# A planner's lengths, weight places and queue order in an attention, MLP and expert kernel

## The chip, the cores and the metric

The kernel runs on one core of a Trainium2 chip. The metric is the device time of one execution in microseconds (us); the time before is 1440.73 us, the median of three runs (1438.99 to 1442.17).

## The reference

Three layers follow each other. Everything is float32.

```
# 1. attention through 32 packed queries, for each of 8 batches x 8 heads (576 tokens, 64 wide)
p_packed = sm_attn(p, k, v)                  # sm_attn: softmax(scale * a @ b.T) @ c
out = sm_attn(q, p_packed, p_packed)
x = out.transpose(0, 2, 1, 3).reshape(4608, 512)
# 2. MLP, 512 -> 2048 -> 512
h = x @ w_in
x = (h * tanh(softplus(h))) @ w_out
# 3. experts: each token goes to the best of 8
logits = x @ w_gate
e_idx = argmax(logits); gate_w = softmax(logits)[e_idx]
eom = sigmoid(x @ w_output_gate)
out[token] = gate_w * eom[e_idx] * (relu(x @ w1[e_idx]) @ w2[e_idx])
```

The weights `w_in` and `w_out` come as 64-bit floats (4 MB and 4 MB of float32 content, loaded as two 32-bit words each) and are converted on the chip into float32 values or into a rounded high and a low part.

## The kernel before, in words

**An order made by a planner.** The program is not written in the order in which it runs. Each step is handed to a class `Order` (line 32) by `od.op(engine, length, function, reads, writes, ...)`. `Order.run` (line 132) is a list scheduler: it keeps a time for each engine, takes among the steps whose inputs are made the one that can start first (a tie goes to the lower `prio`, then to the older step), and calls its function, which emits the instructions. The length, a landing time `lat` for DMAs and a hop of 0.18 us between engines are the only things that it knows of time. They are not waits in the program: the result is one fixed list of instructions for each engine, and the waits among them come from the data. Each engine works its list in order, so an instruction whose input is late holds back all that stands behind it on that engine. Where a step may run on ScalarE or VectorE (a dict of lengths), the planner chooses the engine too. Steps carry a group number; a step more than `AHEAD` = 3 groups in front of the oldest unfinished group is held back.

`Order.place` (line 100) gives each buffer one of the places of its tag, the one that comes free first. Places of different tags may overlap in memory; a place is taken only when every buffer that overlaps it has been read for the last time. The weight words have eight places `raw`, in the memory that the packed products `wp` use later.

When the planner sees TensorE pause between two steps, `Order.fill` (line 117) puts filler matmuls (function `busy`, line 432 in the profile) into the pause, one for each 0.25 us, on a bank that is free. Their results are not used.

**The stages.** A *unit* (function `unit`, line 498) is the attention of four heads of one batch: 16 units, two for each batch. It loads K, the packed queries (two DMAs), V and Q over SP's queue, transposes K on TensorE (`heads_T`), forms the scores of the packed queries, takes their softmax (line 584 is the Exp on ScalarE), multiplies by V, and then the second softmax over the 32 packed keys. Unit 1 has buffers and PSUM banks of its own (5 and 6); all other units share one set (banks 0 and 1) and follow each other. Line 535 is the first transpose of a unit, line 637 the transpose after which the packed result `pt_b` is known, line 731 its last matmuls.

`convert` (line 762) loads a block of weights (512 KB) over SP (line 772), one step on ScalarE (line 779), four on VectorE (788, 791, 797, 803), and sums on TensorE (821 to 824). There are 32 such blocks, four for each of four column groups of `w_in` (`i`) and of `w_out` (`o`).

`packed(b)` (line 844) multiplies the packed result of batch b with `w_in`: four matrices (line 855) one after another through one buffer `wq`, which takes banks 0 and 1 together. Each is then evacuated in four steps (two high parts, two low parts) into two of the eight places `wp`.

`block(j)` (line 876) is one of 18 blocks of 256 tokens, each with eight *pairs* (`pair`, line 889): a first product (line 909 from the packed matrices, line 900 for the two blocks of leftover tokens), the activation in nine steps on ScalarE, VectorE and GpSimd (913, 916, 944, 948, 954), and a second product (line 930). Batch b uses blocks `FIRST[b]` and `FIRST[b] + 1`. `route` then chooses the expert of each token (its count matmul is line 1029) and stores the rows.

`slot` (line 1213) is one of 16 slices of 288 tokens of one expert: rows gathered, expert weights loaded over SP and split (1273, 1276), products 1328, 1362 and 1370, and the scatter of the result. They begin near 960 us.

**What sets the order around the change.** `LO` lists the loads of SP's queue by preference (`u` the five loads of a unit, `c` a block of `convert`). `UAT` gives the group of each unit, `CPR` the priority of the steps of each four blocks of `convert`. Units have priority -2 to -4, `packed` -1, the first product of a pair 0 and the second 1.

Of the kernel before, what the change touches and what calls it, by code (L numbers as in the profile page):

```python
# [14 lines left out]
AF = mybir.ActivationFunctionType  # L15
# [174 lines left out]
def tile_attn_moe_moe(  # L190
# [36 lines left out]
    CW = 512  # L227
# [93 lines left out]
    def banks(*n):  # L321
# [18 lines left out]
        tab0=area(PT, 264), tab1=area(XT + 1024, 720), zero=area(ROW, E * CAP // 128),  # L340
        xl0=area(XL, 1024), xl1=area(XT + 1024, 1024), wp=area(WP, 1024, 8), raw=area(WP, 1024, 8), wq=[(("b", 0, 1), ("b", 1, 1))],
        Lx=area(WP + 8192 - LS, LS), tu=area(CT, 512, 2), ts=area(CT + 1024, 512, 4),
# [136 lines left out]

    left, at_b, pt_b = {}, {}, {}  # L480
# [10 lines left out]

    LO = ('u u' + 16 * ' c' + 8 * ' c' + ' u' + 8 * ' c' + ' u').split()

# [4 lines left out]
    def unit(u):  # L498
# [5 lines left out]
        def buf(tag):  # L504
            return od.buf(f"{tag}{x}")
# [20 lines left out]

        op("SP", 1.65, lambda: f_ld(k, kn), w=[kn], lat=LAND, at=start)
        for c in range(2):
            op("SP", 0.3, lambda c=c: f_pn(c), m=[pn], lat=LAND, at=start)
        op("SP", 1.65, lambda: f_ld(v, vn), w=[vn], lat=LAND, at=start)  # L530
        op("SP", 1.65, lambda: f_ld(q, qn), w=[qn], lat=LAND, at=start)
# [63 lines left out]
        for r in range(2):  # L595
            op("DVE", 0.38, lambda r=r: f_mx(r), r=[sc], w=[mx])
        op("DVE", 0.13, f_mm, w=[mx])
# [90 lines left out]
        for c in range(2):  # L688
# [3 lines left out]
            op("DVE", d, lambda c=c: f_sub(c), r=[s2[c], sm], w=[a2])  # L692
        op("ACT", 0.65, lambda: A.activation(out=a2.t, in_=a2.t, func=AF.Exp, scale=scale), w=[a2])
        op("DVE", 1.27, f_sum, r=[a2], w=[sm])
        op("Pool", 1.23, lambda: nc.gpsimd.tensor_tensor(
            out=a2.t, in0=a2.t, in1=gb(sm.t[:, 1]), op=ALU.mult), r=[sm], w=[a2])
# [4 lines left out]
        for c in (1, 0):  # L701
# [12 lines left out]
            else:  # L714
# [47 lines left out]
    def convert(n, srcs, dst, part, after=(), at=0.0, prio=0):  # L762

        cc, wb = od.buf("cc"), dst if part else od.buf("raw")

# [43 lines left out]
        lo = at_in("c", n)  # L809
        od.op("SP", 1.46, f_ld, w=[wb], lat=2.0, after=after, at=at, prio=prio if lo is None else lo - 100)  # L810
# [33 lines left out]
    def packed(b):  # L844

        for m in range(DFF // CW):
# [12 lines left out]

            od.op("PE", 0.95, f_w, r=[pt_b[b, 0], pt_b[b, 1]] + [wi_b[h][m] for h in range(4)], w=[wq], prio=WPR)  # L860
            for g in range(2):
# [10 lines left out]

                od.op(dict(ACT=0.48, DVE=0.6), None, f_hi, r=[wq], w=[wp], prio=WPR)
                od.op("DVE", 0.6, f_lo, r=[wq], w=[wp], prio=WPR)

# [13 lines left out]
    def pair(j, i, i0, i1, acc):  # L889
# [49 lines left out]
        else:  # L939
            need = [x for g in range(2) for x in (at_b[b, g], wp_b[b, i // 2, g])]  # L940
        last["g1", j] = od.op("PE", 3.5 if b is None else 1.31, f_g1, r=need, w=[hps], prio=0, after=())
        if b is not None and half and i == KF // 2 - 1:
            free_at[b] = [last["g1", j]]
        od.op("ACT", 0.49, lambda: A.activation(  # L944
            out=tl(tu, [128, 2, TB]), in_=hps.t, func=AF.Tanh, scale=0.5), r=[hps], w=[tu])
        od.op("ACT", 0.53, f_ts, r=[tu], w=[ts])
        od.op("ACT", 0.53, lambda: sq(tu.t, ts.f, QA, QB), r=[ts], w=[tu])
        od.op("ACT", 0.53, lambda: A.activation(out=tu.t, in_=tu.t, func=AF.Exp, bias=QC), w=[tu])  # L948
        od.op("DVE", 0.61, lambda: stt(ts.f, ts.f, 0.5, tu.t), r=[tu], w=[ts])
        od.op("ACT", 0.53, lambda: sq(ts.f, ts.f, 1.0, -1.5), w=[ts])  # L950
        od.op("DVE", 0.61, lambda: stt(ts.f, ts.f, 0.75, tu.t), r=[tu], w=[ts])
        od.op("DVE", 0.61, lambda: stt(ts.f, ts.f, -1.0, hps.t), r=[hps], w=[ts])
# [3 lines left out]
        last["g2", j] = od.op("PE", 2.59, f_g2, r=[g, ts] + wo_b[2 * i:2 * i + 2], w=[acc], prio=1, after=left[final(1)] if j == 0 and i == 0 else ())  # L956

    def route(j, acc, part):
# [254 lines left out]
    def slot(od, mem, j, dram_b, marks, early=False):  # L1213
# [70 lines left out]
        for i in range(8):  # L1284
            op("SP", 1.5, lambda i=i: f_raw(i), "x0", r=[tab[0]], w=[raw[i]], lat=4.0)
        for i in range(8):
            late = 0 if i > 3 else 0.0
            op("ACT", 0.96, lambda i=i: f_wh(i), r=[raw[i]], w=[ws[i]], pen=pen + late)
            op("DVE", 1.14, lambda i=i: f_wl(i), r=[raw[i]], w=[ws[i]], pen=pen + late)

# [3 lines left out]
        for kk in range(KD):  # L1294
# [208 lines left out]
```

## Time and profile before

| | us |
|---|---|
| median of three runs | 1440.73 |
| the profiled execution | 1453.15 |
| its span (first to last instruction) | 1451.4 |
| TensorE busy | 1394.5 |
| VectorE busy | 1040.5 |
| ScalarE busy | 845.4 |
| GpSimd busy | 413.3 |

The profile is of one execution. PE is TensorE's matmuls, PEld its weight loads, DVE is VectorE, ACT ScalarE, POOL GpSimd, and SP the engine whose queue issues most DMAs. L930 is line 930 of the kernel. Filler counts as busy time of PE. PEclk is the granted clock of TensorE as a share of its full speed. "Idle before, releaser" names the instruction that a waiting one waited for last.

### The profile page before, as it was taken

The page shows a single profiled execution, that of the slowest core. Times are in us where ns is not written, and L with a number is a line of the kernel's source. Part 1 is how long each engine was busy: PE and PEld are TensorE (multiplying, and loading weights), DVE is VectorE, ACT ScalarE, POOL GpSimd, SP SyncE. Part 2 cuts the span into 40 slices and gives each one's busy share as a digit, 9 for nine tenths or more (in the row PEclk, how much of TensorE's full clock was granted, in tenths as well). Part 3 has the DMA queues.
Part 4 walks back from the last instruction along what each step waited for, and adds up shares of the span by engine and source line. Part 5 has one row for each costly group of instructions (what it writes and reads, how often), then busy time and mean ns, then how long its engine had stood idle before and what let it go on. Part 6 is the DMA issues. An engine that isn't in the chain of part 4 may idle for free.

```text
span 1451.4 us, 25837 instructions
## 1 busy us (share of the span) xinstructions
PE 1394.5 (96%) x9594; PEld 1094.8 (75%) x9594; DVE 1040.5 (72%) x2312; ACT 845.4 (58%) x1631; POOL 413.3 (28%) x388
## 2 busy tenths in 40 slices
PE   7789999999999999999999999999999999999997
PEld 4457676777876787887678788778778788878886
DVE  4789777787866856885787887767677767767653
ACT  3568555786756756775777777654354444435432
POOL 1122032233322323332233333431432223223111
PEclk9999999999999999999999999999999999999999
DMA  9871123212223103132210121543654664565430
GB/s 243 206 199 27 35 50 70 62 34 48 41 55 70 34 17 50 16 66 61 57 16 18 16 15 16 147 88 140 198 209 157 194 228 165 177 219 194 150 141 27
DMA packets 70134, 143.61 MB, mean 99 GB/s; under 512 B 13552, under 2 KB 32112, under 8 KB 70000
## 3 DMA queue, kind: packets, MB, share of 16 engines
q1 hardware_dynamic: 61680, 122.92, 32.1%
q0 software_dynamic: 8320, 18.96, 3.9%
q8 instruction: 77, 1.26, 0.5%
q14 instruction: 57, 0.47, 0.1%
HBM read 122.77 MB, written 19.08 MB: 98 GB/s over the span
## 4 chain that ended last, share of the span: by engine, by line
PE 69%; DVE 12%; issue 7%; ACT 5%; DMA 4%; POOL 1%; another core or an unknown queue 1%; SPq 0%; POOLq 0%; DVEq 0%; ACTq 0%
PE b L930 22%; PE b L1328 11%; PE b L1362 10%; PE b L909 9%; DVE f L916 5%; PE b L900 3%; DMA f<-in_moe_w_in_dram 2%; ACT f L913 2%; PE b L855 2%; PE b L1299 2%; PE b L1370 2%; PE b L547 2%; PE b L432 1%; PE b L980 1%; PE b L564 1%
## 5 line engine op out<-in xcount | busy, mean ns | idle before, releaser
L930 PE MATMUL b<-r,r 128*128 128x512 f32 x1728 | 430.3, 400 | 4.9 <-POOL r L954 4.9
L930 PEld LDWEIGHTS b<-r,r 128*128 128x128 f32 x1728 | 317.4, 189 | 80.3 <-issue 8.4
L954 POOL TENSOR_TENSOR r<-f,r 128x512 fp32r<-128x512 f32 x144 | 199.5, 1386 | 468.6 <-ACT r L440 216.6
L913 ACT ACTIVATE f<-f 128x512 f32<-128x512 f32 x432 | 264.6, 628 | 87.2 <-DVE f L916 56.2
L916 DVE SCALAR_TENSOR_TENSOR f<-f,f 128x512 f32<-128x512 f32 x288 | 234.0, 817 | 77.1 <-ACT f L913 44.7
L1328 PE MATMUL b<-r,r 128*128 128x288 f32 x1536 | 213.6, 297 | 4.8 <-issue 3.3
L1328 PEld LDWEIGHTS b<-r,r 128*128 128x128 f32 x1536 | 208.9, 190 | 9.3 <-issue 4.7
L909 PE MATMUL b<-r,r 128*128 128x256 f32 x1536 | 206.8, 286 | 3.1 <-DVE f L916 2.9
L909 PEld LDWEIGHTS b<-r,r 128*128 128x128 f32 x1536 | 189.0, 190 | 24.3 <-DVE f L916 8.8
L1362 PE MATMUL b<-r,r 128*128 128x512 f32 x768 | 191.8, 399 | 0.0
L1362 PEld LDWEIGHTS b<-r,r 128*128 128x128 f32 x768 | 140.3, 188 | 37.2 <-issue 7.5
L1276 DVE TENSOR_TENSOR r<-f,r 128x1024 fp32r<-128x1024 f32 x128 | 157.3, 1241 | 10.3 <-ACT r L1273 7.7
L440 ACT ACTIVATE f<-b 128x288 f32<-128x288 f32 (+5 forms) x229 | 101.2, 464 | 71.4 <-PE b L637 20.4
L1273 ACT ACTIVATE r<-f 128x1024 fp32r<-128x1024 f32 x128 | 132.7, 1056 | 12.8 <-DMA f<-in_moe_w_dram 8.9
L1389 POOL DMA_INDIRECT out_dram<-f,f x48 | 51.2, 1066 | 286.6 <-ACT f L1378 164.7
L944 ACT ACTIVATE f<-b 128x512 f32<-128x512 f32 x144 | 85.1, 591 | 59.6 <-DVE f L916 28.8
L1335 ACT ACTIVATE r<-b 128x288 fp32r<-128x288 f32 x95 | 38.8, 410 | 117.3 <-PE b L1328 99.0
L916 DVE SCALAR_TENSOR_TENSOR f<-f,b 128x512 f32<-128x512 f32 x144 | 98.2, 683 | 3.5
L948 ACT ACTIVATE f<-f 128x512 f32<-128x512 f32 x144 | 90.5, 628 | 2.5
L440 ACT ACTIVATE r<-b 128x512 fp32r<-128x512 f32 (+1 forms) x119 | 59.3, 509 | 37.6 <-PE b L824 12.6
L442 DVE COPY f<-b 128x288 f32<-128x288 f32 (+5 forms) x115 | 57.8, 516 | 32.7 <-PE b L564 17.2
L1378 ACT ACTIVATE f<-b,f 128x512 f32<-128x512 f32 x26 | 17.9, 688 | 94.9 <-PE b L1362 90.1
(181 smaller groups left out, 1638.5 us busy)
## 6 DMA issues: line engine op xcount, KB each, us to landing
f<-in_moe_w_dram SPq DMA_DIRECT2D x128, 512.0 KB
xr<-f SPq DMA_DIRECT2D x36, 257.0 KB
f<-in_k_dram SPq DMA_DIRECT2D x16, 576.0 KB
f<-in_v_dram SPq DMA_DIRECT2D x16, 576.0 KB
f<-in_q_dram SPq DMA_DIRECT2D x16, 576.0 KB
f<-in_moe_w_in_dram SPq DMA_DIRECT2D x32, 256.0 KB
f<-in_moe_w_out_dram SPq DMA_DIRECT2D x16, 512.0 KB
f<-in_p_dram SPq DMA_DIRECT2D x32, 32.0 KB
```

The costliest lines, as they stand in the source:

```text
L440: A.activation(out=dst, in_=src, func=AF.Copy)
L909: nc.tensor.matmul(t[:, c, :], lhsT=wt, rhs=xx, start=(n == 0), stop=(n == 5))
L913: A.activation(out=out, in_=in_, func=AF.Square, scale=sc, bias=b)
L916: V.scalar_tensor_tensor(out=out, in0=in0, scalar=s, in1=in1, op0=ALU.add, op1=ALU.mult)
L930: nc.tensor.matmul(acc.t[t], lhsT=gg[:, c, sl], rhs=wo_at(f, ww), start=(f == 2 * i0 and n == 0), stop=(f == 2 * i1 - 1 and n == 2),)
L944: od.op("ACT", 0.49, lambda: A.activation(out=tl(tu, [128, 2, TB]), in_=hps.t, func=AF.Tanh, scale=0.5), r=[hps], w=[tu])
L948: od.op("ACT", 0.53, lambda: A.activation(out=tu.t, in_=tu.t, func=AF.Exp, bias=QC), w=[tu])
L954: od.op(LOE, None, lambda eng: either(eng).tensor_tensor(out=ts.t, in0=ts.f, in1=g.t.bitcast(F32), op=ALU.subtract), r=[g], w=[ts])
L1273: A.activation(out=wpart(i, 0), in_=raw[i].t, func=AF.Copy)
L1276: V.tensor_tensor(out=wpart(i, 1), in0=raw[i].t, in1=wpart(i, 0).bitcast(F32), op=ALU.subtract)
L1328: nc.tensor.matmul(t, lhsT=ww[:, sl], rhs=xpart(x)[:, kk], start=(n == 0), stop=(n == 3 * KD - 1))
L1362: nc.tensor.matmul(bank(ps), lhsT=h[x], rhs=w[y], start=(f == 0 and n == 0), stop=(f == KE - 1 and n == 2))
```

## The change

Most lengths that the planner is given become longer, and one (a copy on VectorE) shorter; a load on SP is booked by its size, 2.13 us for 512 KB and 2.35 us for 576 KB, and lands 7 us later (`LAND`) where weight loads had 2 us before. Weight blocks that belong to the first two column groups of `w_in` may take four more places, in the memory of the last two column groups. The order of the blocks, the order of the loads on SP and the priorities of the blocks change; unit 3 moves to group 0. From batch 2 on, the first transposes of a unit (packed queries, K and Q) are ordered behind the last matrix of `packed` of the batch in front, and units of later groups are handed to the planner after `packed`. The numbers and shapes of the instructions stay.

```diff
@@ slots
-  raw=area(WP, 1024, 8), wq=...
+  raw=area(WP, 1024, 8), raw0=area(WI + 4096, 1024, 4) + area(WP, 1024, 8), wq=...
@@ lengths (us)
-    HIE = {'ACT': 0.53, 'DVE': 0.6}
-    HR = dict(ACT=0.09, DVE=0.1)
-    YO = dict(ACT=0.57, DVE=0.6)
-    LOE = {'Pool': 1.24}
+    HIE = {'ACT': 0.63, 'DVE': 0.56}
+    HR = dict(ACT=0.19, DVE=0.19)
+    YO = dict(ACT=0.68, DVE=0.7)
+    LOE = {'Pool': 1.38}
-    EV = dict(ACT=0.3, DVE=0.38)
+    EV = dict(ACT=0.44, DVE=0.48)
@@ order of loads on SP
-    LO = ('u u' + 16 * ' c' + 8 * ' c' + ' u' + 8 * ' c' + ' u').split()
+    LO = ('u u' + 16 * ' c' + 8 * ' c' + 8 * ' c' + ' u u').split()
@@ unit
-        op("SP", 1.65, lambda: f_ld(k, kn), w=[kn], lat=LAND, at=start)
+        op("SP", 2.35, lambda: f_ld(k, kn), w=[kn], lat=LAND, at=start)
...
+        begun = made.get(b - 1, ()) if b > 1 else ()
         op("PE", 0.12, lambda: nc.tensor.transpose(bank(pt)[:, 0:128], ...),
-           r=[pn], w=[pt])
+           r=[pn], w=[pt], after=begun)
...
-                op("PE", 0.25, f, r=[src], w=[t_ps])
+                op("PE", 0.25, f, r=[src], w=[t_ps], after=begun)
@@ convert
-        cc, wb = od.buf("cc"), dst if part else od.buf("raw")
+        early = [wi_b[kk][m] for kk in range(KD) for m in range(2)]
+        cc, wb = od.buf("cc"), dst if part else od.buf("raw0" if dst in early else "raw")
...
-        od.op("SP", 1.46, f_ld, w=[wb], lat=2.0, ...)
-        op("ACT", 0.53, f_a1, r=[wb], w=[cc])
-        op("DVE", 0.34, f_b1, w=[cc])
-        op("DVE", 0.61, f_sg, w=[cc])
-        op("DVE", 0.34, f_pw, w=[cc])
-        op("DVE", 0.61, f_lw, r=[wb], w=[cc])
+        od.op("SP", 2.13, f_ld, w=[wb], lat=LAND, ...)
+        op("ACT", 0.67, f_a1, r=[wb], w=[cc])
+        op("DVE", 0.43, f_b1, w=[cc])
+        op("DVE", 0.69, f_sg, w=[cc])
+        op("DVE", 0.43, f_pw, w=[cc])
+        op("DVE", 0.69, f_lw, r=[wb], w=[cc])
@@ packed
-            od.op("PE", 0.95, f_w, ..., w=[wq], prio=WPR)
+            made[b] = [od.op("PE", 0.95, f_w, ..., w=[wq], prio=WPR)]
@@ pair
-        last["g1", j] = od.op("PE", 3.5 if b is None else 1.31, f_g1, ...)
+        last["g1", j] = od.op("PE", 3.5 if b is None else 1.39, f_g1, ...)
...
-        last["g2", j] = od.op("PE", 2.59, f_g2, ...)
+        last["g2", j] = od.op("PE", 2.78, f_g2, ...)
@@ slot
-            op("SP", 1.5, lambda i=i: f_raw(i), "x0", ..., lat=4.0)
+            op("SP", 2.13, lambda i=i: f_raw(i), "x0", ..., lat=4.0)
...
-            cop("PE", 1.475, f_g1, "g1", r=[xx] + ws[0:4], w=[ps])
+            cop("PE", 1.6, f_g1, "g1", r=[xx] + ws[0:4], w=[ps])
@@ the loop over blocks
-    UAT = [0, 0, 0, 1, 2, 2, 4, 4, 6, 6, 8, 8, 11, 11, 13, 13]
+    UAT = [0, 0, 0, 0, 2, 2, 4, 4, 6, 6, 8, 8, 11, 11, 13, 13]
...
-        for u in units.get(j, ()):
-            od.group = j
-            unit(u)
         if j == 0:
+            for u in units[0]:
+                od.group = j
+                unit(u)
             od.group = None
-            n, CPR = 0, [0, 0, 0, 0, 1, 1, 1, 1]
-            for kind, m in [(x, m) for m in range(DFF // CW) for x in 'io']:
+            n, CPR = 0, [0] * 8
+            for kind, m in [('i', 0), ('i', 1), ('o', 0), ('i', 2), ('o', 1), ('i', 3), ('o', 2), ('o', 3)]:
...
         if j in PAT:
             packed(PAT[j])
+        for u in units.get(j, ()) if j else ():
+            unit(u)
```

## Rows read from the trace of the kernel before

**Rows 1.** The page's busy time of each engine: us (share of the span) xinstructions.
```profile
PE 1394.5 (96%) x9594; PEld 1094.8 (75%) x9594; DVE 1040.5 (72%) x2312; ACT 845.4 (58%) x1631; POOL 413.3 (28%) x388
```

**Rows 2.** Stages, all instructions: from:to, length, busy us of each engine, clock, DMA.
```profile
22.70:56.30 33.60, 30.20 (x279) 16.52 (x279) 30.72 (x66) 17.09 (x37) 4.76 (x6) 0.95 1.04 277
...
62.10:84.00 21.90, 21.62 (x165) 13.64 (x165) 19.76 (x45) 17.48 (x37) 3.68 (x2) 0.88 0.84 210
84.00:88.90 4.90, 0.02 (x2) 0.02 (x1) 4.90 (x10) 2.60 (x5) 4.83 (x1) 0.87 1.01 306
88.90:110.00 21.10, 21.10 (x109) 15.21 (x109) 14.20 (x30) 11.88 (x23) 1.94 (x2) 0.87 0.58 147
...
204.00:262.00 58.00, 55.75 (x451) 37.61 (x450) 41.40 (x119) 32.27 (x70) 12.58 (x12) 1.00 0.26 52
262.00:417.00 155.00, 153.03 (x1227) 122.53 (x1226) 122.84 (x272) 117.18 (x234) 53.20 (x45) 1.00 0.23 47
417.00:462.00 45.00, 42.70 (x358) 29.21 (x357) 27.75 (x74) 25.16 (x54) 9.58 (x10) 1.00 0.30 67
...
650.00:706.00 56.00, 53.78 (x429) 37.41 (x428) 35.10 (x89) 32.88 (x70) 11.79 (x11) 1.00 0.26 60
...
1064.00:1400.00 336.00, 336.00 (x2060) 280.75 (x2059) 234.95 (x456) 154.19 (x279) 90.36 (x87) 1.00 0.55 185
```

**Rows 3.** The same for line 432 (filler) alone: busy us of PE and PEld.
```profile
0.00:110.00 110.00, 22.26 (x79) 7.72 (x79) 0.91 0.87 216
...
204.00:262.00 58.00, 10.87 (x42) 3.86 (x42) 1.00 0.26 52
262.00:417.00 155.00, 0.98 (x4) 0.12 (x2) 1.00 0.23 47
417.00:462.00 45.00, 7.38 (x28) 2.58 (x28) 1.00 0.30 67
...
650.00:706.00 56.00, 7.38 (x28) 2.59 (x28) 1.00 0.26 60
...
sum 1451.40, PE 56.15 PEld 18.96; mean PE 7.02 PEld 2.37
```

**Rows 4.** Waits of TensorE up to 200 us: us in total, times, longest.
```profile
PE b L731 <- DVE f L442: 5.8, 1, 5.8
PE b L607 <- ACT f L584: 5.7, 1, 5.7
PE b L930 <- POOL r L954: 4.9, 1, 4.9
```

**Rows 5.** ScalarE in order of time near 21 us: start, length, what, idle before.
```profile
21.48 0.66 ACT L779 ACTIVATE f<-f 128x512 f32<-128x512 f32 x1 [5.51 <-DMA f<-in_moe_w_in_dram]
22.04 0.48 ACT L584 ACTIVATE f<-b,f 128x288 f32<-128x288 f32 x1
```

**Rows 6.** Waits of SP's queue up to 130 us: total, times, longest.
```profile
SPq L772 <- DVE r L803: 24.6, 5, 12.8
SPq L523 <- PE b L535: 23.8, 2, 18.8
```

**Rows 7.** TensorE in order of time, unit 4's first transpose, then 248 to 257 us.
```profile
174.68 0.27 PE L535 MATMUL b<-ident,f 128*128 128x128 f32 x1
...
248.41 1.59 PE L855 MATMUL b<-f,f 64*32 64x512 f32 x16
249.94 2.12 PE L432 MATMUL b<-ones 128*128 128x512 bf16 x9
251.98 1.37 PE L855 MATMUL b<-f,f 64*32 64x512 f32 x16
253.28 3.01 PE L909 MATMUL b<-r,r 128*128 128x256 f32 x24
```

**Rows 8.** Lines 731 and 1029: min/median/max ns, first and last start in us.
```profile
L731 PE MATMUL b<-f,f x128: 222/222/368, 45.9 to 812.7; 128*64 128x64 f32 x128
L1029 PE MATMUL b<-f,tri x18: 166/179/180, 209.7 to 1016.1; 128*128 128x8 bf16 x18
```

More of the change, by code (lines that the diff above doesn't have):

```diff
@@ L340, in tile_attn_moe_moe @@
         tab0=area(PT, 264), tab1=area(XT + 1024, 720), zero=area(ROW, E * CAP // 128),
-        xl0=area(XL, 1024), xl1=area(XT + 1024, 1024), wp=area(WP, 1024, 8), raw=area(WP, 1024, 8), wq=[(("b", 0, 1), ("b", 1, 1))],
+        xl0=area(XL, 1024), xl1=area(XT + 1024, 1024), wp=area(WP, 1024, 8), raw=area(WP, 1024, 8), raw0=area(WI + 4096, 1024, 4) + area(WP, 1024, 8), wq=[(("b", 0, 1), ("b", 1, 1))],
         Lx=area(WP + 8192 - LS, LS), tu=area(CT, 512, 2), ts=area(CT + 1024, 512, 4),
@@ L477, in f_wgl @@
         )
-    left, at_b, pt_b = {}, {}, {}
+    left, at_b, pt_b, made = {}, {}, {}, {}
     xl_b = [od.buf(f"xl{i}") for i in range(2)]
@@ L525, in f_pn @@
             )
-        op("SP", 1.65, lambda: f_ld(k, kn), w=[kn], lat=LAND, at=start)
+        op("SP", 2.35, lambda: f_ld(k, kn), w=[kn], lat=LAND, at=start)
         for c in range(2):
-            op("SP", 0.3, lambda c=c: f_pn(c), m=[pn], lat=LAND, at=start)
-        op("SP", 1.65, lambda: f_ld(v, vn), w=[vn], lat=LAND, at=start)
-        op("SP", 1.65, lambda: f_ld(q, qn), w=[qn], lat=LAND, at=start)
+            op("SP", 0.5, lambda c=c: f_pn(c), m=[pn], lat=LAND, at=start)
+        op("SP", 2.35, lambda: f_ld(v, vn), w=[vn], lat=LAND, at=start)
+        op("SP", 2.35, lambda: f_ld(q, qn), w=[qn], lat=LAND, at=start)
+        begun = made.get(b - 1, ()) if b > 1 else ()
         pt, bd = buf("pp"), buf("bd")
         op("PE", 0.12, lambda: nc.tensor.transpose(bank(pt)[:, 0:128], pn.t.rearrange("p c d -> p (c d)"), ident),
-           r=[pn], w=[pt])
+           r=[pn], w=[pt], after=begun)
         op(dict(ACT=0.16, DVE=0.2), None, lambda eng: evac(eng, tl(bd, [128, 128]), pt.t[:, 0:128]), r=[pt], w=[bd])
@@ L595, in unit @@
         for r in range(2):
-            op("DVE", 0.38, lambda r=r: f_mx(r), r=[sc], w=[mx])
+            op("DVE", 0.45, lambda r=r: f_mx(r), r=[sc], w=[mx])
         op("DVE", 0.13, f_mm, w=[mx])
@@ L692, in unit @@
             op("DVE", d, lambda c=c: f_sub(c), r=[s2[c], sm], w=[a2])
-        op("ACT", 0.65, lambda: A.activation(out=a2.t, in_=a2.t, func=AF.Exp, scale=scale), w=[a2])
+        op("ACT", 0.73, lambda: A.activation(out=a2.t, in_=a2.t, func=AF.Exp, scale=scale), w=[a2])
         op("DVE", 1.27, f_sum, r=[a2], w=[sm])
-        op("Pool", 1.23, lambda: nc.gpsimd.tensor_tensor(
+        op("Pool", 1.39, lambda: nc.gpsimd.tensor_tensor(
             out=a2.t, in0=a2.t, in1=gb(sm.t[:, 1]), op=ALU.mult), r=[sm], w=[a2])
@@ L809, in convert @@
         lo = at_in("c", n)
-        od.op("SP", 1.46, f_ld, w=[wb], lat=2.0, after=after, at=at, prio=prio if lo is None else lo - 100)
-        op("ACT", 0.53, f_a1, r=[wb], w=[cc])
-        op("DVE", 0.34, f_b1, w=[cc])
-        op("DVE", 0.61, f_sg, w=[cc])
-        op("DVE", 0.34, f_pw, w=[cc])
-        op("DVE", 0.61, f_lw, r=[wb], w=[cc])
+        od.op("SP", 2.13, f_ld, w=[wb], lat=LAND, after=after, at=at, prio=prio if lo is None else lo - 100)
+        op("ACT", 0.67, f_a1, r=[wb], w=[cc])
[3 more added lines that the diff above has]
+        op("DVE", 0.69, f_lw, r=[wb], w=[cc])
         cv = od.buf("cv")
@@ L858, in f_w @@
                         )
-            od.op("PE", 0.95, f_w, r=[pt_b[b, 0], pt_b[b, 1]] + [wi_b[h][m] for h in range(4)], w=[wq], prio=WPR)
+            made[b] = [od.op("PE", 0.95, f_w, r=[pt_b[b, 0], pt_b[b, 1]] + [wi_b[h][m] for h in range(4)], w=[wq], prio=WPR)]
             for g in range(2):
@@ L871, in f_lo @@
                     )
-                od.op(dict(ACT=0.48, DVE=0.6), None, f_hi, r=[wq], w=[wp], prio=WPR)
-                od.op("DVE", 0.6, f_lo, r=[wq], w=[wp], prio=WPR)
+                od.op(dict(ACT=0.59, DVE=0.68), None, f_hi, r=[wq], w=[wp], prio=WPR)
+                od.op("DVE", 0.68, f_lo, r=[wq], w=[wp], prio=WPR)
     def block(j, i0=0, i1=KF // 2):
@@ L940, in pair @@
             need = [x for g in range(2) for x in (at_b[b, g], wp_b[b, i // 2, g])]
-        last["g1", j] = od.op("PE", 3.5 if b is None else 1.31, f_g1, r=need, w=[hps], prio=0, after=())
+        last["g1", j] = od.op("PE", 3.5 if b is None else 1.39, f_g1, r=need, w=[hps], prio=0, after=())
         if b is not None and half and i == KF // 2 - 1:
             free_at[b] = [last["g1", j]]
-        od.op("ACT", 0.49, lambda: A.activation(
+        od.op("ACT", 0.6, lambda: A.activation(
             out=tl(tu, [128, 2, TB]), in_=hps.t, func=AF.Tanh, scale=0.5), r=[hps], w=[tu])
[L946 to L952, printed above, removed]
+        od.op("ACT", 0.63, f_ts, r=[tu], w=[ts])
+        od.op("ACT", 0.63, lambda: sq(tu.t, ts.f, QA, QB), r=[ts], w=[tu])
+        od.op("ACT", 0.63, lambda: A.activation(out=tu.t, in_=tu.t, func=AF.Exp, bias=QC), w=[tu])
+        od.op("DVE", 0.77, lambda: stt(ts.f, ts.f, 0.5, tu.t), r=[tu], w=[ts])
+        od.op("ACT", 0.63, lambda: sq(ts.f, ts.f, 1.0, -1.5), w=[ts])
+        od.op("DVE", 0.77, lambda: stt(ts.f, ts.f, 0.75, tu.t), r=[tu], w=[ts])
+        od.op("DVE", 0.69, lambda: stt(ts.f, ts.f, -1.0, hps.t), r=[hps], w=[ts])
         last["hi", j] = od.op(HIE, None, lambda eng: evac(eng, tl(g, [128, 2, TB], F32R), ts.f), r=[ts], w=[g])
@@ L955, in pair @@
             out=ts.t, in0=ts.f, in1=g.t.bitcast(F32), op=ALU.subtract), r=[g], w=[ts])
-        last["g2", j] = od.op("PE", 2.59, f_g2, r=[g, ts] + wo_b[2 * i:2 * i + 2], w=[acc], prio=1, after=left[final(1)] if j == 0 and i == 0 else ())
+        last["g2", j] = od.op("PE", 2.78, f_g2, r=[g, ts] + wo_b[2 * i:2 * i + 2], w=[acc], prio=1, after=left[final(1)] if j == 0 and i == 0 else ())
     def route(j, acc, part):
@@ L1284, in slot @@
         for i in range(8):
-            op("SP", 1.5, lambda i=i: f_raw(i), "x0", r=[tab[0]], w=[raw[i]], lat=4.0)
+            op("SP", 2.13, lambda i=i: f_raw(i), "x0", r=[tab[0]], w=[raw[i]], lat=4.0)
         for i in range(8):
             late = 0 if i > 3 else 0.0
-            op("ACT", 0.96, lambda i=i: f_wh(i), r=[raw[i]], w=[ws[i]], pen=pen + late)
-            op("DVE", 1.14, lambda i=i: f_wl(i), r=[raw[i]], w=[ws[i]], pen=pen + late)
+            op("ACT", 1.06, lambda i=i: f_wh(i), r=[raw[i]], w=[ws[i]], pen=pen + late)
+            op("DVE", 1.23, lambda i=i: f_wl(i), r=[raw[i]], w=[ws[i]], pen=pen + late)
         def xpart(x):
@@ L1311, in slot @@
             cop(EV, None, f_xh, "dx", r=[ps], w=[xx], front=True)
-            cop("DVE", 0.38, f_xl, r=[ps], w=[xx], front=True)
+            cop("DVE", 0.45, f_xl, r=[ps], w=[xx], front=True)
         hT, hr = [], od.buf("hr")
```

12 lines of the change are left out of this document (6 added, 6 removed).

## The prediction

> **What bounds the kernel now.** I read the busy shares first. TensorE counts as busy for 1394.5 us of the span of 1451.4, VectorE for 1040.5, ScalarE for 845.4 [rows 1]; so a new order of the same work can win only what TensorE does not spend on work. That has two parts: idle time, and the filler matmuls of line 432, which the planner puts into every pause that it foresees on TensorE; they took 56.15 us in all [rows 3]. 1451.4 − (1394.48 − 56.15) = 113 us without work. Then the stage table with all instructions [rows 2] against the same stages with the filler alone [rows 3]: idle time of TensorE is the stage less its busy time, and idle plus filler is dead time.
> - From 1064 to 1400 TensorE has no idle moment in 336 us [rows 2]; nothing can be won there.
> - The stretches 204–262, 417–462 and 650–706 hold 2.25 + 10.87 = 13.1, 2.30 + 7.38 = 9.7 and 2.22 + 7.38 = 9.6 us of dead time: 32.4 in 159 us. The stretch between the first two holds 1.97 + 0.98 = 2.95 in 155 us; two others like it lie behind (462–650, 706–904).
> - The first 110 us hold three true stalls of TensorE, 5.7, 5.8 and 4.9 us [rows 4], and stages with a granted clock of 0.95, 0.88 and 0.87 [rows 2].
>
> What ended the waits says why. At 22 us TensorE waits for the second Exp of unit 0 (line 584), and that instruction stands on ScalarE behind a weight conversion (line 779), which sat 5.51 us until its words landed [rows 5]: the planner had booked a weight load at 1.46 us plus 2.0 to land. At 62 us it is the same with line 442 on VectorE, behind line 788. In SP's queue, loads of raw weight words wait 24.6 us in all for line 803 to free a place, 12.8 us once, and unit 3's packed queries wait up to 18.8 us for unit 2's transpose [rows 6] with every later load behind them. In the dead stretches the PE rows show filler between the matrices of `packed` (line 855), and the pairs that need them (line 909) only after the last [rows 7]. Attention has priority -2, `packed` -1, and a `wq` takes banks 0 and 1 together, which attention takes one by one.
>
> **The change, part by part.** The trace is of an execution of 1453.15 us, 12.4 above the median of 1440.73. I work out savings in its time and take them off the median; 0.9% of a saving of tens of us is nothing.
>
> *Lengths.* The program has the same instructions, and no length is a wait: they only steer the planner. The new ones stand near the rows (line 779 is booked at 0.67 instead of 0.53; it took 0.66 [rows 5]). Where TensorE never idles (1064–1400) the order was already good enough; I put this at 0 there. Elsewhere longer chains in the model can show it more pauses and so more filler: from −8 us (the filler outside the first 110 us and the three bad stretches: 56.15 − 22.26 − 25.63 [rows 3]) to +10 (as much again). I take 0, the nearer stages being smooth.
>
> *Loads by bytes, landing 7 us, four more raw places, new load order.* This is the first 110 us. The stall up to 22.7 (5.7 us [rows 4]) goes, since the planner now books the first words late and lets the Exp go first; but the unit then waits sooner for its own next step: I count 4. The stall up to 62.1 (5.8) goes whole: all 32 weight blocks now stand on SP ahead of the five loads each (K, two of the packed queries, V, Q) of units 2 and 3, so nothing of unit 3 blocks that queue, and the twelve places (eight before) take the first eight blocks of `w_in` at once. Of the 4.9 us at 84–88.9 I count 1.9 only, for VectorE was busy in all of it [rows 2]: there it is the engine that bounds, and 32 conversions of about 2.2 us on it (4 steps at 0.43 and 0.69, as booked now) are 72 us that no order removes. The clock lost 33.6 × 0.05 + 21.9 × 0.12 + 21.1 × 0.13 = 7.0 us of work in the stages behind the stalls; I count 3.3 back. Sum 15.0. Against it: unit 2 is loaded behind eight more weight blocks (4 MB) than before, and `packed` of batch 1 needs units 2 and 3; and with CPR all zero a late weight block no longer yields to pairs. Bounds for that: 0 (unit 3 had all 32 in front of it before too) and 5.8 (one more stall like that at 56 us); I take 4, nearer the stall, since VectorE has no slack to catch up. **First term: 11 us** less, bounds 0 and 23.3 (16.3 of stalls and 7.0 of clock).
>
> *Attention behind the matrix in front.* `begun` makes the transposes of unit 2b and 2b+1 wait, in the planner, for the last matrix of batch b−1. It is an order on TensorE's queue and adds no instruction. Unit 3 is made in group 0 instead of 1, which only lifts a limit. The order takes away what held `wq` back. At the rate of the smooth stretch, 2.95/155, the 159 us of the three bad stretches would have 3.0 dead, so 29.4 are in excess. Of those about half lie between the matrices themselves: each next one waits until four evacuations of about 0.6 us have emptied both banks, and that stays when no pair is at hand. So 14.7. What waits now: both units of a batch, and behind them `packed` of the same batch, which needs the second unit up to about two fifths of its chain. Units follow each other at (812.7 − 45.9)/15 = 51 us, blocks at (1016.1 − 209.7)/17 = 47 [rows 8]; 1.4 units are 72 us and two blocks 95, so it fits with 23 us to spare. I take 1.7 off for the tight ones. **Second term: 13 us** less, bounds 29.4 less and 40 more (below).
>
> Sum: 11 + 13 = 24; 1440.7 − 24 = **1417 us**.
>
> One rule of the Trainium skill speaks against the second term (TensorE: Matmul & The Clock Gate, section "HAM oscillation — how this bites in real kernels"): a kernel that lets TensorE wait long in each round starts each round on the slow clock. The trace agrees: behind the stall at 56–62 the granted clock was 0.88, that is partly at 1.2 GHz, while the bad stretches, with filler in their pauses, kept 1.00 [rows 2, 3]. It is the last rival below.
>
> **Rivals.**
> - *Only the start is won* (0.17): the dead time between the matrices is the emptying of banks 0 and 1 and not attention in front. For it: in rows 7 the filler lies between two matrices with nothing of attention between. Against it: the smooth transitions empty the same banks. 1440.7 − 11 = 1430 us.
> - *All stalls go* (0.10): 23.3 + 29.4 less, and some filler back: about 1392 us. Against it: VectorE is full at the start.
> - *Nothing moves* (0.08): VectorE sets the start whatever the order, and what the transitions give, new filler takes: 1441 us, within 0.2% (2.9 us, about what a measurement can tell from no change).
> - *Attention comes late* (0.15), the slower side: one mechanism, the same `begun`. From the point where 1.4 units last longer than the two blocks in which they must run (units of 68 us, against 51 now), `packed` is late at every batch. For it: no unit may now begin before the last matrix, where before some began some 77 us ahead (unit 4 at 174.7, against the matrix at 252 [rows 7]); against it the 23 us to spare. Price: the second term is lost, and the four smooth transitions get an excess of half a bad one each (29.4/3/2 = 5) to a whole one: +20 to +40; with the first term 1450 to 1470 us; say 1452.
> - *Pauses without filler* (0.05): the model sees no pause where there still is one, so none is filled, and the clock falls at each of seven transitions. By the row at 62–84 a fall costs 2.6 us of work: +18 − 11, 1448 us.
>
> **How the numbers follow.** Forecast as reasoned 0.45, with its own range 1400 to 1430. Faster by over 0.2%: 0.45 + 0.17 + 0.10 = 0.72; within 0.2%: 0.08; slower: 0.15 + 0.05 = 0.20. The range to hold 8 in 10 leaves out the end of "all stalls go" and the dear half of "attention comes late": 1396 to 1450.
>
> **What would show it.** In the first term: no wait of TensorE over 4 us before 100 us, both Exps of unit 0 ahead of the first line 779 on ScalarE, SP's wait for line 803 well under 24.6 us, no granted clock under 0.9 in a stage after 30 us. In the second: the four matrices of each batch from 1 on within about 20 us, no unit's first transpose ahead of the last matrix of the batch in front, filler from 200 to 900 us under 12 us (it is 27 or so now). It would be wrong if line 855 waits for line 442 or 637 of a late unit, if TensorE idles more than now between 200 and 900, or if the stretch behind 1064 lengthens.

## The result, and the profile after

The changed kernel takes 1415.62 us (median of four runs, 1414.34 to 1416.88), against 1439.86 us of the kernel before, measured beside it; the ratio is 0.9827, 95% interval 0.9803 to 0.985. The forecast was 1417 us.

The page of the changed kernel, busy time of each engine, answers to [rows 1]. TensorE is busy for 98% of a span that is 36 us shorter. The kernels' work is the same, but the planner moved 60 instructions from ScalarE to VectorE, and there is more filler: 65.7 us instead of 56.1 in the two traces compared below.

```profile
PE 1385.3 (98%) x9646; PEld 1089.7 (77%) x9646; DVE 1057.3 (75%) x2372; ACT 826.3 (58%) x1571; POOL 424.3 (30%) x388
```

Some 12 of these 36 us are not the change's. The kernel before took 1443 us on two of the chips and 1457 us on another; the trace that the prediction read (1453.15 us) is like the slower one. Its stretch behind the last count matmul (1016 to the end) lasted 435 us, where a second trace of the same kernel has 427. So I read the terms from two traces taken on one chip, the kernel before again (1441.18 us) and the changed one again (1419.92 us, the slowest of its four executions). Their spans differ by 21.3 us; by medians on that chip the two kernels differ by 27.0 us.

Stages of the kernel before: up to the count matmul of block 0, from there to that of block 17, and the rest; all instructions, then the filler alone. Columns as in [rows 2].

```profile
0.00:207.70 207.70, 182.83 (x1300) 121.71 (x1301) 158.75 (x330) 122.44 (x244) 42.45 (x62) 0.95 0.53 133
207.70:1012.60 804.90, 790.12 (x5740) 620.99 (x5740) 597.88 (x1399) 540.06 (x1051) 252.01 (x213) 1.00 0.26 52
1012.60:1439.50 426.90, 416.32 (x2557) 348.69 (x2556) 282.78 (x585) 182.41 (x336) 119.45 (x113) 0.99 0.52 175
...
0.00:207.70 207.70, 24.00 (x85) 8.21 (x85) 0.95 0.53 133
207.70:1012.60 804.90, 29.89 (x112) 10.14 (x112) 1.00 0.26 52
1012.60:1439.50 426.90, 2.21 (x7) 0.60 (x7) 0.99 0.52 175
```

The same stages of the changed kernel:

```profile
0.00:199.20 199.20, 189.45 (x1366) 120.70 (x1367) 169.39 (x342) 126.27 (x249) 39.05 (x61) 1.00 0.51 133
199.20:986.60 787.40, 776.60 (x5712) 620.12 (x5710) 601.91 (x1438) 517.25 (x995) 253.53 (x215) 1.00 0.28 54
986.60:1418.20 431.60, 420.05 (x2572) 349.66 (x2571) 285.27 (x593) 182.26 (x328) 129.12 (x113) 0.99 0.53 173
...
0.00:199.20 199.20, 37.29 (x144) 13.29 (x144) 1.00 0.51 133
199.20:986.60 787.40, 22.48 (x90) 8.13 (x90) 1.00 0.28 54
986.60:1418.20 431.60, 5.96 (x22) 1.74 (x22) 0.99 0.53 173
```

| us | before: length, idle + filler, clock | changed |
|---|---|---|
| to block 0 | 207.7, 24.9 + 24.0 = 48.9, 0.95 | 199.2, 9.8 + 37.3 = 47.0, 1.00 |
| to block 17 | 804.9, 14.8 + 29.9 = 44.7, 1.00 | 787.4, 10.8 + 22.5 = 33.3, 1.00 |
| the rest | 426.9, 10.6 + 2.2 = 12.8, 0.99 | 431.6, 11.6 + 6.0 = 17.5, 0.99 |

Dead time is idle time plus filler. The reader is to see three things. In the first stage the idle time fell by 15.1 us and the filler rose by 13.3: the dead time is nearly the same, and what was won is the clock. A clock of 0.95 on 207.7 us loses 10.4 us, which is an upper bound for the work, since it counts idle time and filler too; busy time without filler fell by 6.6 us, from 158.8 to 152.2, though the changed kernel does a little more work there (1222 matmuls, where 1215 were). In the second stage the dead time fell by 11.4. In the third it rose by 4.7, as the stage did. Dead time and clock together (106.3 to 97.8 us; a mean clock of 0.989 on 1439.5 us lost 15.8, one of 0.995 on 1418.2 loses 7.1) give 17.2 of the 21.3 us. The other 4 us I can't place: the second stage's busy time without filler fell by 6.1 us at a clock that both rows show as 1.00.

Each stage ends at the same instruction, but the planner moves other work across that point; so between versions dead time can be compared by stage, and the length of a stage only where about as many matmuls stand in it.

What ended the waits has changed too. ScalarE near 16 us in the first trace of the changed kernel (start, length): all Exps of units 0 and 1 (line 585 now) stand ahead of the first conversion (line 781 now), where one stood behind it in [rows 5].

```profile
15.68 0.50 ACT L585 ACTIVATE f<-b,f 128x288 f32<-128x288 f32 x1 [2.11 <-DVE f L580]
...
16.18 0.49 ACT L585 ACTIVATE f<-b,f 128x288 f32<-128x288 f32 x1
...
22.87 0.50 ACT L585 ACTIVATE f<-b,f 128x288 f32<-128x288 f32 x1 [0.36 <-DVE f L580]
...
23.36 0.49 ACT L585 ACTIVATE f<-b,f 128x288 f32<-128x288 f32 x1
...
24.31 0.68 ACT L781 ACTIVATE f<-f 128x512 f32<-128x512 f32 x1
```

The longest waits of TensorE up to 200 us (total, times, longest), against [rows 4]:

```profile
PE b L823 <- DVE r L805: 2.7, 4, 1.3
PE b L432 <- DVE cb L259: 1.1, 1, 1.1
```

TensorE in order of time at the matrices of batch 1 (line 857 now), against [rows 7]: four matrices within 25 us with pairs (line 911) between them, no filler, and unit 4's first transpose (line 536) behind the last.

```profile
152.16 1.09 PE L857 MATMUL b<-f,f 64*32 64x512 f32 x16
153.18 1.65 PE L911 MATMUL b<-r,r 128*128 128x256 f32 x12
...
163.28 1.09 PE L857 MATMUL b<-f,f 64*32 64x512 f32 x16
...
168.63 1.09 PE L857 MATMUL b<-f,f 64*32 64x512 f32 x16
...
175.36 1.09 PE L857 MATMUL b<-f,f 64*32 64x512 f32 x16
...
184.77 0.27 PE L536 MATMUL b<-ident,f 128*128 128x128 f32 x1
```

The bad stretches of [rows 2] were those around the matrices of batches 1, 3 and 5. In the changed kernel the matrices stand elsewhere, so the rows to read are those around its own: batch 1 (150 to 185), the stretch behind block 0 (200 to 274), batch 3 (382 to 403) and batch 7 (811 to 840), all from the second trace, then the filler alone.

```profile
150.00:185.00 35.00, 35.00 (x248) 26.65 (x247) 29.19 (x47) 25.97 (x47) 10.64 (x8) 1.00 0.00 1
200.00:274.00 74.00, 67.86 (x539) 55.17 (x538) 54.96 (x141) 44.15 (x90) 23.00 (x20) 0.95 0.31 56
...
382.00:403.00 21.00, 20.92 (x178) 11.83 (x177) 15.94 (x54) 12.46 (x24) 3.26 (x3) 1.00 0.02 6
...
811.00:840.00 29.00, 28.82 (x225) 17.63 (x224) 23.95 (x64) 17.39 (x33) 5.83 (x5) 1.00 0.13 20
...
150.00:185.00 35.00, 0.00 (x0) 0.00 (x0) 1.00 0.00 1
200.00:274.00 74.00, 1.19 (x4) 0.38 (x4) 0.95 0.31 56
...
382.00:403.00 21.00, 7.13 (x32) 2.88 (x32) 1.00 0.02 6
...
811.00:840.00 29.00, 11.50 (x47) 4.28 (x47) 1.00 0.13 20
```

Batch 1 has no dead time, nor have batches 2, 4 and 5 (274–303, 473–504, 587–625); batch 6 has 1.2 us (706–732). Batch 3 has 7.2 us and batch 7 11.7, nearly all of it filler between and beside their matrices; in the kernel before, the matrices of batch 7 (790–830) had 0.3. Behind block 0 there are 6.1 us idle, of which TensorE waits 5.2 for VectorE, which waits for a row store (see e9).

### The profile page after: what moved, and what is told of

The parts are those of the page before. It is cut to its first block, busy times and chain, and to the rows that moved or that the text cites. A ratio compares the mean times of both kernels' runs of the same rounds, so it can differ in the third digit from the quotient of the medians.

```text
span 1415.2 us, 25947 instructions
## 1 busy us (share of the span) xinstructions
PE 1385.3 (98%) x9646; PEld 1089.7 (77%) x9646; DVE 1057.3 (75%) x2372; ACT 826.3 (58%) x1571; POOL 424.3 (30%) x388
## 4 chain that ended last, share of the span: by engine, by line
PE 80%; DVE 8%; issue 7%; DMA 2%; POOL 1%; ACT 1%; POOLq 0%; ACTq 0%; DVEq 0%; SPq 0%
PE b L932 26%; PE b L911 12%; PE b L1330 10%; PE b L1364 9%; PE b L902 3%; PE b L432 3%; PE b L857 2%; PE b L548 2%; DVE f L918 2%; PE b L1301 2%; PE b L1372 1%; PE b L823 1%; PE b L982 1%; PE b L565 1%; PE b L620 1%
## 5 line engine op out<-in xcount | busy, mean ns | idle before, releaser
L932 PEld LDWEIGHTS b<-r,r 128*128 128x128 f32 x1728 | 316.1, 189 | 72.6 <-issue 7.0
L918 DVE SCALAR_TENSOR_TENSOR f<-f,f 128x512 f32<-128x512 f32 x288 | 228.7, 800 | 67.1 <-ACT f L915 42.6
L1330 PE MATMUL b<-r,r 128*128 128x288 f32 x1536 | 208.1, 295 | 0.0
L1330 PEld LDWEIGHTS b<-r,r 128*128 128x128 f32 x1536 | 205.6, 188 | 2.0
L911 PEld LDWEIGHTS b<-r,r 128*128 128x128 f32 x1536 | 188.1, 188 | 23.6 <-issue 11.7
L1278 DVE TENSOR_TENSOR r<-f,r 128x1024 fp32r<-128x1024 f32 x128 | 154.4, 1216 | 3.1 <-ACT r L1275 3.1
L1391 POOL DMA_INDIRECT out_dram<-f,f x48 | 47.8, 995 | 277.1 <-ACT f L1380 173.4
L440 ACT ACTIVATE f<-b 128x288 f32<-128x288 f32 (+5 forms) x184 | 84.0, 466 | 72.8 <-PE b L826 13.2
L442 DVE COPY f<-b 128x288 f32<-128x288 f32 (+5 forms) x160 | 81.1, 522 | 42.4 <-PE b L548 15.1
L1337 ACT ACTIVATE r<-b 128x288 fp32r<-128x288 f32 x84 | 34.5, 412 | 69.3 <-PE b L1330 67.0
```

The costliest lines, as they stand in the source:

```text
L440: A.activation(out=dst, in_=src, func=AF.Copy)
L911: nc.tensor.matmul(t[:, c, :], lhsT=wt, rhs=xx, start=(n == 0), stop=(n == 5))
L918: V.scalar_tensor_tensor(out=out, in0=in0, scalar=s, in1=in1, op0=ALU.add, op1=ALU.mult)
L932: nc.tensor.matmul(acc.t[t], lhsT=gg[:, c, sl], rhs=wo_at(f, ww), start=(f == 2 * i0 and n == 0), stop=(f == 2 * i1 - 1 and n == 2),)
L1278: V.tensor_tensor(out=wpart(i, 1), in0=raw[i].t, in1=wpart(i, 0).bitcast(F32), op=ALU.subtract)
L1330: nc.tensor.matmul(t, lhsT=ww[:, sl], rhs=xpart(x)[:, kk], start=(n == 0), stop=(n == 3 * KD - 1))
```

## The experiments

Three parts: the *start part* (load order, block order and priorities, raw places, SP bookings), the *order at the matrices* (`begun`, units handed over after `packed`), the *lengths* of the other steps. Unit 3 stands in group 0 in every run but e6. All ratios are to the kernel before, measured beside each, with 95% intervals. e1 to e4 ran on the slow chip. The lengths alone were not run, and within the start part the order of the loads was not parted from that of the blocks.

| run | parts in it | ratio |
|---|---|---|
| e1 | start | 1.0084 (1.0051 to 1.0117) |
| e7 | order at the matrices | 0.9936 (0.9912 to 0.996) |
| e2, e12 | start, order | 0.9795 (0.9761 to 0.9829), 0.9784 (0.9765 to 0.9802) |
| e3 | start, lengths | 0.9882 (0.9859 to 0.9905) |
| e4 | order, lengths | 0.9944 (0.9926 to 0.9963) |
| e5 | all | 0.9819 (0.9796 to 0.9843) |
| e8 | all, no filler | 0.9901 (0.9873 to 0.993) |
| e9 | all, old load and block order, eight places | 0.9992 (0.9978 to 1.0007) |
| e10 | all, old SP bookings | 0.9908 (0.9888 to 0.9928) |
| e11 | all, eight places | 0.982 (0.9796 to 0.9843) |

**e1, the start part alone.**

```diff
-    LO = ('u u' + 16 * ' c' + 8 * ' c' + ' u' + 8 * ' c' + ' u').split()
+    LO = ('u u' + 16 * ' c' + 8 * ' c' + 8 * ' c' + ' u u').split()
-        od.op("SP", 1.46, f_ld, w=[wb], lat=2.0, ...)
+        od.op("SP", 2.13, f_ld, w=[wb], lat=LAND, ...)
...
```

> The kernel before with the start part alone: load order on SP, order and priorities of the weight blocks, four more raw places, SP lengths and landing time of the loads of units and weights, unit 3 in group 0; not the order behind the matrix in front, not the lengths of the engines' steps. Theory A (the start order gives some 11 us, the order behind the matrix some 13, lengths nothing): 1429 us, granted clock of the first 110 us at 1.00 as after, bad stretches at the matrices of packed still there (some 30 us of dead time between 200 and 710). Rival B (the lengths give nearly all, the planner only needed true durations): 1438 to 1441 us. Rival C (the parts need each other): 1436 or more.

1467.14 us, slower. The start itself became the shorter for it (first row below: 187.5 us to block 0, clock 1.00, though with less work in it, 1144 matmuls besides the filler), but the second stage took 835.0 us with 26.4 us idle and 46.4 of filler (second row, and the filler's row). That is 72.8 us of dead time, 27 more than in the first trace of the kernel before (45.9), which is like this chip. The `w_in` blocks stand earlier in the new order, and batch 0's fourth matrix stood at 130.7 us, where the second trace of before has it at 165.2. The units were not earlier: unit 2's first transpose stood at 100.5 us (62.0 before), unit 3's at 140.8 (124.4). The first matrix of batch 1 came at 173.2 us (207.9 before), and units 4 and 5 began between it and the last, as the lines of TensorE show. Five batches of seven have units between their matrices in e1, three before. Why the planner puts more of them there when the matrices can start earlier was not tested. Stages as above, then TensorE in order of time:

```profile
0.00:187.50 187.50, 176.57 (x1266) 113.55 (x1267) 152.91 (x314) 125.03 (x246) 34.59 (x60) 1.00 0.52 139
187.50:1022.50 835.00, 808.60 (x5857) 629.60 (x5852) 598.11 (x1404) 545.59 (x1052) 252.97 (x214) 0.99 0.28 49
...
187.50:1022.50 835.00, 46.36 (x184) 15.92 (x184) 0.99 0.28 49
```

```profile
173.20 1.10 PE L856 MATMUL b<-f,f 64*32 64x512 f32 x16
...
181.84 0.33 PE L535 MATMUL b<-ident,f 128*128 128x128 f32 x1
...
217.51 1.17 PE L856 MATMUL b<-f,f 64*32 64x512 f32 x16
218.61 2.33 PE L432 MATMUL b<-ones 128*128 128x512 bf16 x10
220.87 1.40 PE L856 MATMUL b<-f,f 64*32 64x512 f32 x16
...
228.82 0.33 PE L535 MATMUL b<-ident,f 128*128 128x128 f32 x1
...
254.16 1.59 PE L856 MATMUL b<-f,f 64*32 64x512 f32 x16
```

**e7, the order at the matrices alone.**

```diff
+        begun = made.get(b - 1, ()) if b > 1 else ()
...
-           r=[pn], w=[pt])
+           r=[pn], w=[pt], after=begun)
...
```

> The kernel before with the order behind the matrix in front alone (units handed over after packed, unit 3 in group 0 as that needs it; lengths, load order and places of before). Theory A (the order at the matrices is worth 13 us or more by itself): ratio 0.990 or less, dead time from the end of block 0 to block 17 about 33 us instead of 46. Rival C (it gives what it gives only with the early loads of units 2 and 3, since without them the units are late and packed waits): ratio 0.997 to 1.01.

1433.29 us, faster by 0.64%, between theory A, which asked for 1% or more, and rival C. Dead time from block 0 to block 17 was 37.1 us, where the kernel before had 44.7 on that chip. The start stayed as it was (205.6 us, clock 0.93).

**e2 and e12, both, with the lengths of before.** The lines of e1 and e7 together.

> The changed kernel with the engine lengths of before (start part and order behind the matrix in front kept). Theory A: as the changed kernel, 1416 us, within 3 us; dead time of 200 to 710 us under 17 us. Rival B (lengths): 1430 us or more. If lengths add filler only: 1413 us or less.

> Start part and order behind the matrix in front with the engine lengths of before, a second time and in more rounds. If the engine lengths are worth nothing where the other two are in: 0.980 to 0.984, as the changed kernel (0.9827 and 0.9819). If they cost: 0.979 or less, and this version beats both.

1426.8 us on the slow chip, 1412.65 on a fast one, and the best ratio of all. Together the two give 2.1%, where one alone loses 0.8% and the other wins 0.6%: with the lengths of before, the new start pays only when the units can't go between the matrices. In e12 the start took 191.0 us, 8 less than in the changed kernel, of which 3.8 are dead time; the rest is work that the planner put behind block 0 (1159 matmuls besides the filler stand in front, 1222 in the changed kernel). The dead time of the three stages was 43.2, 32.4 and 12.3:

```profile
0.00:191.00 191.00, 180.07 (x1281) 114.85 (x1281) 155.45 (x318) 127.58 (x249) 34.55 (x60) 1.00 0.50 135
191.00:978.90 787.90, 772.88 (x5727) 615.89 (x5719) 601.25 (x1425) 528.03 (x1024) 253.24 (x214) 1.00 0.29 53
978.90:1410.90 432.00, 422.21 (x2589) 353.11 (x2588) 285.04 (x586) 184.48 (x344) 119.11 (x114) 0.99 0.54 177
...
0.00:191.00 191.00, 32.27 (x122) 11.01 (x122) 1.00 0.50 135
191.00:978.90 787.90, 17.39 (x64) 5.49 (x64) 1.00 0.29 53
978.90:1410.90 432.00, 2.46 (x9) 0.72 (x9) 0.99 0.54 177
```

**e3, the changed kernel without the order at the matrices.**

```diff
-        begun = made.get(b - 1, ()) if b > 1 else ()
...
-           r=[pn], w=[pt], after=begun)
+           r=[pn], w=[pt])
...
```

> The changed kernel without the order behind the matrix in front (the units' transposes may go before it again, and later units are handed over ahead of packed as before). Theory A: 1429 us, with three or more bad stretches of some 10 us dead time at the matrices. Rival B (lengths): 1416 us, since true lengths alone bring the matrices in time. Rival C: above 1436 us.

1438.53 us. The three bad stretches are there (14.5, 8.7 and 9.1 us dead in 204–262, 417–462 and 650–706), and the second stage holds 42.6 us of dead time. Against e1, on the same chip, the lengths won 28.6 us: where nothing else holds the units back, the longer lengths do much of what the order does.

**e4, the changed kernel without the start part.** The lines of e1 taken back.

> The changed kernel without the start part (old load order, old order and priorities of weight blocks, eight raw places, loads booked 1.46 us and landing 2 us). Theory A: 1427 us, with true stalls of TensorE of about 5 us each in the first 100 us and a granted clock near 0.9 there. Rival B: 1418 us, since the lengths of the steps were what set the order of the start. Rival C: above 1436 us.

1447.76 us. To block 0 it took 220.7 us with 21.5 us idle, 47.1 of filler and a clock of 0.95. Longer lengths with the old bookings make the start longer than before (209.7 us in the trace of before that is like it); the gain is in the second stage (35.3 us dead, where 45.9 were).

**e5, the changed kernel again.**

> The changed kernel once more, beside the parts. If start part plus order behind the matrix (ratio 0.9795 to the kernel before) is all that the change gives, this one is at 0.980 too; if the longer engine lengths give something of their own, at 0.975 or less; if they cost something (filler put in where the longer chains show pauses, 65 us of it against 56 us), at 0.983.

1416.33 us, as first measured. With e12 at 0.9784 it is rather the last case: the lengths cost something of their own. The two intervals touch, but e11, whose TensorE does as the changed kernel's, was measured beside e12: its executions took 1414.56 to 1419.6 us, those of e12 1410.39 to 1413.9. The dead time is 97.8 us against 87.9, with 3.8 of the difference in the start and 5.3 behind block 17, where e12 has 30 more matmuls and the stage is as long (432.0 and 431.6 us).

**e6, the kernel before again.** No edit.

> The kernel before, unchanged, for a second profile: does the trace that the prediction was made from show what the kernel does each time? Expected: the three bad stretches (some 10 us of dead time each at the matrices of packed), the three true stalls in the first 100 us and the low clock behind them are there again; what differs in span stands in the clock or in waits for DMA.

1441.18 us. The three bad stretches (13.8, 8.6 and 8.6 us dead), the three stalls (5.3, 4.9 and 4.8) and the clock of 0.95 are there again. What differed most from the first trace was the last stage.

**e8, the changed kernel without filler.**

```diff
-    od = Order({**slots, **slots_d}, ahead=AHEAD, busy=busy if 1 else None)
+    od = Order({**slots, **slots_d}, ahead=AHEAD, busy=None)
```

> The changed kernel without the filler matmuls of line 432 (their results are not used). If the filler fills real pauses and holds the clock (the first term came through it): the pauses of the first 110 us are true idle time, granted clock there about 0.9, time 10 to 20 us above the changed kernel (ratio 0.990 to 0.997 to the kernel before). If filler stands in the way of work that was ready: 5 us or more below it (ratio 0.980 or less).

1428.69 us, 12.4 more than the changed kernel on that chip, though 65.7 us of matmuls were gone. Its first stage, against the same row of the changed kernel above, shows why: 205.4 us, 33.7 of them idle, and the clock at 0.95.

```profile
0.00:205.40 205.40, 171.73 (x1222) 114.48 (x1223) 167.81 (x342) 126.48 (x249) 44.16 (x61) 0.95 0.48 129
```

Idle time of the whole was 1428.1 − 1355.5 = 72.6 us, 25 less than the dead time with filler. But the work itself took 1355.5 us instead of 1320.4, 35 more; the mean clock of 0.979 instead of 0.995 explains 0.016 × 1428 = 23 us of that, and the other 12 I can't place. The balance is 10 us in the filler's favour between the two traces, 6.2 of them before block 0, and 12.4 by the medians.

**e9, booking without order.**

```diff
-    LO = ('u u' + 16 * ' c' + 8 * ' c' + 8 * ' c' + ' u u').split()
+    LO = ('u u' + 16 * ' c' + 8 * ' c' + ' u' + 8 * ' c' + ' u').split()
-            n, CPR = 0, [0] * 8
+            n, CPR = 0, [0, 0, 0, 0, 1, 1, 1, 1]
...
```

> The changed kernel with the old load order, old order and priorities of the weight blocks and eight raw places; of the start part only the SP lengths and the landing time of 7 us stay. If the booking is what brings the start (the planner sees when words land, keeps late conversions from standing ahead of ready work, and fills the pauses that it sees): ratio 0.982 to 0.986 to the kernel before, idle time of TensorE up to block 0 under 10 us, clock there 1.00. If order and places bring it: 0.994, as the changed kernel without the whole start part.

1441.55 us: nothing is left of the gain. The expected signs of the booking came (9.0 us idle, clock 1.00 up to block 0), but the stage took 214.1 us with 57.4 of filler: a planner that sees the late words fills the pause and does not shorten it. Behind block 0 came a new stall. The wait of VectorE (line 976, the rows of block 1), SP in order of time, and two waits of SP:

```profile
DVE f L976 <- DMA xr<-f: 12.4, 1, 12.4
```

```profile
218.11 0.33 SPq L518 DMA_DIRECT2D f<-in_k_dram  x1
219.52 0.82 SPq L1089 DMA_DIRECT2D xr<-f  x2
```

```profile
SPq L518 <- PE b L620: 13.0, 1, 13.0
...
SPq L1089 <- DVE f L1083: 1.0, 1, 1.0
```

The load of a unit's K waited 13.0 us for line 620 to free its buffer and was issued 1.4 us ahead of the store of block 0's rows, which itself waited only 1.0 us, for line 1083. The rows of block 1 use the same buffer, and their wait for the store ended at 238.0 us, 18.5 after its issue; the median row store of this run landed after 8.9. Whether the load just in front slowed the store down was not tested.

**e10, order without booking.**

```diff
-        od.op("SP", 2.13, f_ld, w=[wb], lat=LAND, ...)
+        od.op("SP", 1.46, f_ld, w=[wb], lat=2.0, ...)
...
```

> The changed kernel with the old SP lengths and the weight words booked to land after 2 us; the new order of loads and blocks and the twelve places stay. If order and places bring the start: 0.982 to 0.986, without true stalls of 4 us or more in the first 100 us. If the booking does: 0.992 to 0.996, with stalls of 4 us and more behind late conversions and a clock near 0.95 up to block 0.

1430.62 us. The stall behind the late conversion is back (first line, waits of TensorE in the first 100 us), unit 2's first transpose waits for its packed queries to land (second line), and the clock up to block 0 is 0.95 again:

```profile
PE b L608 <- ACT f L585: 5.4, 1, 5.4
PE b L536 <- DMA f<-in_p_dram: 5.2, 1, 5.2
```

So both are needed: the order (1.7% between e9 and the changed kernel) and the booking (0.9% between e10 and it). Up to block 0, e9 took 14.5 us and e10 9.4 us longer than e11 (199.6 us) on the same chip; the rest of e9's loss is behind block 0.

**e11, eight raw places.**

```diff
-        cc, wb = od.buf("cc"), dst if part else od.buf("raw0" if dst in early else "raw")
+        cc, wb = od.buf("cc"), dst if part else od.buf("raw")
```

> The changed kernel with eight raw places instead of twelve for the first column groups. If the four places matter: the loads on SP stop for line 805 early on, and the ratio is 0.985 or more. If not (VectorE is the slower one there, and words only wait in memory): 0.980 to 0.984, as the changed kernel.

1417.08 us, as with twelve. SP waited 20.1 us for line 805 to free places instead of 14.4, and TensorE did not notice: to block 0 it took 199.6 us.

## Why the prediction was right

The time, the sign and both places were right. One step was wrong in its mechanism, the two terms were mis-sized in opposite directions, and one stall was not foreseen; so the closeness of 1417 to 1415.62 is in part luck.

- *Where the time could be won*: right. Nothing was won behind the first expert slices; the part from block 17 on lost 4.7 us.
- *First term, 11 us*: its signs came (no wait of TensorE over 1.3 us in the first 200 us, the Exps ahead of line 781, SP's wait for the conversions down from 24.6 to 14.4 us), and the stage gave 8.5 us, but not as the prediction put it. "The stall up to 22.7 goes" and "the stall up to 62.1 goes whole" hold for idle time, 15.1 us less, and the third stall, of which I counted 1.9, went too; the step that failed is that a stall that goes becomes work. It became filler, 13.3 us more. The step "I count 3.3 back" of the clock was mis-sized: busy time without filler fell by 6.6 us in the stage, and its clock rose from 0.95 to 1.00. e8 and e10 show it: take the filler or the booking away, and the clock is at 0.95 and the stage 6 to 10 us longer. The four raw places, which I put in this term, do nothing (e11).
- *Second term, 13 us*: dead time of the second stage fell by 11.4 us beside the kernel before, and by 9.3 against e3 (on another chip). The half that I left to the emptying of banks 0 and 1 did not stay where I put it: with pairs between the matrices, batches 1, 2, 4 and 5 have no dead time. It stands at the matrices of batches 3 and 7, 18.9 us, which makes the sum come out. Behind block 0 came a stall that no rival named: the wait for the row store, 6.8 us on VectorE and 5.2 on TensorE in e5.
- *Lengths at 0*: right within its bounds (−8 to +10). With both other parts in, they cost rather than give, about 4 us between e12 and e5; beside the start part alone they gave 28.6 us (e1 to e3).
- *Adding the terms*: it worked by luck. The start part alone costs 10 us by the medians and, put to the order at the matrices, wins some 20 (0.9936 to 0.979); a sum of separate terms has no room for that. Taken out of the finished change one at a time, the start part is worth 1.25% or 18 us (e4), the order 0.6% or 9 us (e3), and the lengths cost about 4 to 5 us (e12): against terms of 11, 13 and 0.
- *The rivals.* "Attention comes late" did not happen: batches 1 to 7 have their four matrices within 15 to 25 us. "Only the start is won" fell with e3. "Pauses without filler" came true in one place only, behind block 0, where the stall lowered the clock to 0.95 (200–274). The forecast "filler from 200 to 900 us under 12 us" was wrong: it was 22.5 from block 0 to 17, against 29.9.

A version better than the changed kernel came out: e12, the old lengths with the rest of the change, 1412.65 us, 0.3% ahead of e11 (1417.08 us) beside it.

## What to carry to other kernels

A list scheduler's landing times decide what stands in front of what in each engine's queue; book loads by what the trace shows before tuning any order, and then change the order too, since booking alone only turned a stall into a planned pause here (e9). When one step needs two banks at once and others take them one by one, try ordering the others behind it by hand; having the inputs of that step ready earlier, with neither this order nor the longer lengths, made the kernel slower (e1). When idle time vanishes from a profile, look whether filler and clock took it, stage by stage, before calling it work.

## What was not expected of the hardware

The same kernel takes 1443 us on two chips and 1457 us on another, with a mean granted clock of 0.988 and 0.987 against 0.985, which is about 4 of the 14 us; the rest is not explained. Two traces from different chips must not be subtracted; ratios to a kernel measured beside it agreed (0.9827 and 0.9819 for the changed kernel).

The filler pays for itself in this kernel: without it the mean granted clock fell from 0.995 to 0.979, that is more time at 1.2 GHz, and the kernel took 12.4 us longer.
